# Float64 weights cut into high and low halves straight from their words, with the clamp on GpSimd, and 3 instead of 5 blocks of w_out in the attention stage

## The chip, the cores and the metric

The kernel runs on one core of a Trainium2 chip. The metric is the device time of one execution in microseconds (us), as the median of three runs. Profiles come from a separate, profiled execution; its own time is given beside its span. TensorE is PE in the profile, VectorE is DVE, ScalarE is ACT, GpSimd is POOL, and SP is the engine that issues most transfers.

## The reference

Three layers follow each other. A retention layer runs over 4 batches, 8 heads, 768 steps and 64 channels. A router then gives each of the 3072 tokens to one of 8 experts, 384 tokens each, in order of the logits, and an expert is two matrices with a ReLU between. Last comes a dense layer with softplus. The weights w_in and w_out of that last layer arrive as float64.

```
state = gamma * state + k_t v_t^T ;  y_t = scale * q_t state     # retention, 8 heads
order = argsort(-(x @ w_gate)) ; each token to its best expert with room (cap 384)
out[mask] = max(x[mask] @ w1[e], 0) @ w2[e]                      # expert e
h = x @ w_in ;  g = max(h, 0) + log1p(exp(-abs(h)))              # softplus
return (g @ w_out).astype(float32)
```

## The kernel before

**Stages.** The attention stage (`Attn.emit`) walks over 24 chunks of 128 tokens. Per chunk PE makes the scores (`qk`, tile `pA`), the output (`y`, tile `pY`), the state (`kv`, tile `pS`) and the transpose with the logits (`xo`, tile `pX`). DVE masks the scores (`at`, L125) and reduces the logits (`L`, L166). ACT evicts `yT`, `xs` and the state and scales the values (`vh`). POOL scales the queries (`qs`, L105), and SP loads and stores. Routing of the first expert follows, and then 8 experts, one after the other: `m1` and `m2` are the expert's two matrices, `f1` and `f2` the dense layer for the same 384 tokens. A float32 product is made of three products of a high and a low half, so each weight block has to be cut (`split_w`: ACT copies the high half `whi`, DVE subtracts for the low half `wlo`).

**The conversion.** The class `Conv` turns float64 words into float32. A float64 is loaded as two 32-bit words: `w0` is the lower one, `w1` the upper one with sign, exponent and 20 bits of the fraction (tile `raw`, two words side by side). `Conv.run` is a generator; each `yield` ends one step, and a step is one DVE instruction with what belongs to it on other engines. The first object works in the attention stage on blocks of 128 x 512 numbers: 16 blocks of w_in, each with two outputs (`wih` and `wil`, the high and low halves), and `kept` blocks of w_out with one output (`wo`). `side(j, part)` asks for steps at three places of a chunk: behind `at` of the next chunk, behind `y`, and at the chunk's end. A second object, `F.late`, works on the other rows of w_out in half blocks of 128 x 256. It takes 8 steps while the first list is routed, and then, in expert 0, 3 or 4 steps behind each item of the plan until it is through.

**The order.** All engines run in the order in which the code is written; nothing is rescheduled. Each engine has its own queue, in which a waiting instruction holds up those behind it.

**The steps before.** For one block: ACT writes the magnitude of `w1` to `cM` (L249), DVE shifts and masks `w1` into `cX` (L250), DVE puts the sign and the top exponent bit back (L256). One block later: DVE zeroes what is too small (L242), takes the exponent (L253), scales the lower word by it (L260) and adds (L269, into `cF`, or straight into `wo`). For blocks of w_in ACT then copies `cF` to the high half (L272), and DVE subtracts that for the low half (L263). The steps of two blocks are interleaved, so that most instructions do not need the result of the one just before them.

Of the kernel before, what the change touches and what calls it, by code (L numbers as in the profile page):

```python
# [9 lines left out]
FT = mybir.dt.float32  # L10
# [3 lines left out]
I32 = mybir.dt.int32  # L14
U32 = mybir.dt.uint32
AF = mybir.ActivationFunctionType
OP = mybir.AluOpType
# [19 lines left out]
def layouts(q, k, v, w1, w_in):  # L37

    B, H, S, D = q.shape
    T = lambda a: a.reshape(B, H // 2, 2, S // 128, 128, D).transpose(0, 3, 2, 5, 1, 4).reshape(-1, 128, 1, 512)  # L40
    R = lambda a: a.transpose(0, 2, 1, 3).reshape(-1, 128, 1, 512)
    qk = np.concatenate([T(q), T(k)], axis=2)
    kv = np.concatenate([R(k), R(v)], axis=2)
# [7 lines left out]
class Attn:  # L51
# [4 lines left out]
    def __init__(self, tc, ctx, ps, qk, kv, w_gate, tab, gqt, ident, L, xd, B, H, S):  # L56
        nc = self.nc = tc.nc
        self.ps = ps
        self.qk_in, self.kv_in, self.gq_in, self.L, self.xd, self.ident = qk, kv, gqt, L, xd, ident
        self.B, self.H, self.S = B, H, S  # L60
        self.NC = S // 128
        self.NCH = B * self.NC
        self.HP = HP = H // 2
        c = ctx.enter_context(tc.tile_pool(name="acst", bufs=1, side="right"))
        self.ld = ctx.enter_context(tc.tile_pool(name="ald", bufs=3, side="right"))
        self.wk = ctx.enter_context(tc.tile_pool(name="awk", bufs=2, side="right"))
        self.t = {}
        self.gq = c.tile([128, self.NC - 1, 512], FT, name="gqt")
        n = tab.shape[1] - 128
        ct = c.tile([128, n], FT, name="ctab")  # L70
        self.load(0, "qk")
        nc.scalar.dma_start(ct, tab[:, 128:])
        self.load(0, "kv")
        nc.scalar.dma_start(ident, tab[:, 0:128])
        self.cm = ct[:, 0:1024].rearrange("p (s a t) -> p s a t", s=2, a=HP)
        self.gk = ct[:, 1024:n].rearrange("p (c h) -> p c h", h=self.H)
        self.load(1)
        self.load(2)
        self.sb = []
        for i in range(2):  # L80
            self.sb.append(c.tile([128, HP, 128], FT, name=f"sbd{i}"))
        self.rx = c.tile([128, HP, 136], FT, name="rx")
        nc.scalar.dma_start(self.rx[:, :, 128:136], w_gate.rearrange("(a p) e -> p a e", p=128))
        self.pS = self.ps.tile([128, HP, 128], FT, name="pS")
# [122 lines left out]
        logits(n - 1)  # L207


TINY = float(np.array([897 << 20], np.int32).view(np.float32)[0])  # L210


class Conv:

    def __init__(self, tc, ctx, W, plan, bufs=3):
        self.nc, self.W, self.plan, self.bufs = tc.nc, W, plan, bufs
        self.st = ctx.enter_context(tc.tile_pool(name="cst", bufs=2, side="right"))
# [7 lines left out]
    def ahead(self, p=0):  # L227
        while self.loaded < min(p + self.bufs - 1, len(self.plan)):
            self.load(self.loaded)
            self.loaded += 1  # L230

    def run(self):

        nc, v, N = self.nc, self.nc.vector, len(self.plan)
        T = lambda name, dt, bufs: self.st.tile([128, self.W], dt, name=name, bufs=bufs)
        b, c = None, None
        for p in range(N + 2):
            self.ahead(p)
            a = None
            if b:  # L240
                q, m, x, l0 = b
                v.scalar_tensor_tensor(m, m, TINY, x.bitcast(FT), op0=OP.is_ge, op1=OP.mult)  # L242
                yield
            if p < N:
                raw = self.raw.pop(p)
                w0, w1 = raw[:, :, 0], raw[:, :, 1]
                M, X = T("cM", FT, 2), T("cX", I32, 2)
                a = p, M, X, w0
                nc.scalar.activation(M, w1.bitcast(FT), AF.Abs)  # L249
                v.tensor_scalar(X, w1, 3, 0x3fffffff, op0=OP.logical_shift_left, op1=OP.bitwise_and)  # L250
                yield
            if b:
                v.tensor_scalar(x, m.bitcast(I32), -0x800000, None, op0=OP.bitwise_and)  # L253
                yield
            if p < N:
                v.scalar_tensor_tensor(X, w1, -0x40000000, X, op0=OP.bitwise_and, op1=OP.bitwise_or)  # L256
                yield
            if b:
                e = x.bitcast(FT)
                v.scalar_tensor_tensor(e, l0.bitcast(U32), 2.0 ** -52, e, op0=OP.mult, op1=OP.mult)  # L260
                yield
            if c:
                v.tensor_tensor(c[1], c[0], c[2].bitcast(FT), op=OP.subtract)  # L263
                c = None
                yield
            if b:
                to = self.plan[q][1]
                F = to[0] if len(to) == 1 else T("cF", FT, 2)
                v.tensor_tensor(F, m, e, op=OP.add)  # L269
                if len(to) == 2:  # L270
                    f = F.rearrange("p (a n) -> p a n", a=4)
                    nc.scalar.activation(to[0], f, AF.Copy)  # L272
                    c = f, to[1], to[0]
                self.made += 1
                yield
            b = a

    def step(self, to=None):

# [15 lines left out]
class Route:  # L295
# [120 lines left out]
    def phase(self, i, slow=True, hum=lambda n: None, fill=lambda l: None):  # L416

        nc, N, E, w = self.nc, self.N, self.E, self.wp
        v = nc.vector
        T = lambda shape, dt, name, **k: w.tile(shape, dt, name=name, **k)  # L420
        gap = range
# [8 lines left out]
        for l, (J, s1, sh, span) in enumerate(() if last else LEVELS):  # L430
            if l:
                lo = T([128, N], I32, "lo")
                v.tensor_scalar(lo, self.ik, sh, span - 1, op0=OP.logical_shift_right, op1=OP.bitwise_and)
# [461 lines left out]
@with_exitstack  # L895
def model(ctx, tc, qk, kv, w_gate, w1, w2, w_in, w_out, tab, gqt, out, B, H, S):
    nc = tc.nc
    ctx.enter_context(tc.manual_schedule())
    nc.scalar.preload_act_table_set("natural_log_exp_and_others")
    pers = ctx.enter_context(tc.tile_pool(name="pers", bufs=1))  # L900
    dram = ctx.enter_context(tc.tile_pool(name="dram", bufs=1, space=bass.MemoryType.DRAM))
    NCH, E = 24, w1.shape[0]
    xd = dram.tile([NCH * 128, 512], FT, name="xd")
    L = pers.tile([128, NCH, E], FT, name="L")
    ident = pers.tile([128, 128], FT, name="identp")
    wih = pers.tile([128, 4, 2048], FR, name="wih")
    wil = pers.tile([128, 4, 2048], FR, name="wil")
    wo = pers.tile([128, 16, 512], FT, name="wo")
    holder = {}
    R = Route(tc, pers, None, lambda: holder["ps"](), L, NCH, E)  # L910
    w_in, w_out = w_in.bitcast(I32), w_out.bitcast(I32)
    c0, c1, c2 = (ctx.enter_context(ExitStack()) for _ in range(3))
    aps = c0.enter_context(tc.tile_pool(name="aps", bufs=1, space=bass.MemoryType.PSUM))
    cuts = [(w_in[f], (wih[:, :, f * 128:(f + 1) * 128], wil[:, :, f * 128:(f + 1) * 128])) for f in range(16)]
    kept = 5
    rows = [w_out[f * 128:(f + 1) * 128] for f in range(16)]
    cuts += [(rows[f], (wo[:, f],)) for f in range(kept)]
    cv = Conv(tc, c1, 512, cuts)
    a = Attn(tc, c2, aps, qk, kv, w_gate, tab, gqt, ident, L, xd, B, H, S)

    def side(j, part):
        cv.step((3 * j + part) * 144 // 71)

    def logits(j):
        if j % 6 == 5:
            R.first_part(j - 5, j + 1)

    a.emit(side, logits)
    cv.step(1000)
    c2.close()  # L930
    c1.close()
    R.wp = ctx.enter_context(tc.tile_pool(name="rwork", bufs=1, reuse_waits="tile"))
    holder["ps"] = lambda: a.ps.tile([128, 512], FT, name="pS")
    F = Ffn(tc, R, w1, w2, (wih, wil), [wo[:, f, :] for f in range(16)], xd, out, ident)
    F.open0(ctx)
    halves = [(rows[f][:, h * 512:h * 512 + 512], (wo[:, f, h * 256:h * 256 + 256],))
              for f in range(kept, 16) for h in range(2)]
    F.late, F.kept = Conv(tc, ctx, 256, halves, 3), kept
    F.start(a.ps.tile([128, 2, 4, 128], FT, name="pA", bufs=2)[:, 0].rearrange("p a t -> p (a t)"))
    c0.close()  # L940
    F.open(ctx)
    holder["ps"] = lambda: F.rps.tile([128, 512], FT, name="rt")
    F.emit()
# [25 lines left out]
```

## Time and profile before

| | |
|---|---|
| time, median of 3 runs | 1062.14 us (1061.06 to 1062.66) |
| profiled execution, its time | 1059.53 us |
| its span | 1057.8 us |
| PE busy | 1003.0 us (95%) |
| DVE busy | 694.6 us (66%) |
| ACT busy | 575.4 us (54%) |
| POOL busy | 84.1 us (8%) |

The shares are averages over stages with different limits, so they are to be read stage by stage. The attention stage ends near 144 us of the span, the routing of the first expert near 175 us, and the second conversion works until about 275 us. A busy share counts an instruction from its start to its end, also where it is held up inside; two instructions of one engine can overlap a little.

### The profile page before, as it was taken

The page shows a single profiled execution, that of the slowest core. Times are in us where ns is not written, and L with a number is a line of the kernel's source. Part 1 is how long each engine was busy: PE and PEld are TensorE (multiplying, and loading weights), DVE is VectorE, ACT ScalarE, POOL GpSimd, SP SyncE. Part 2 cuts the span into 40 slices and gives each one's busy share as a digit, 9 for nine tenths or more (in the row PEclk, how much of TensorE's full clock was granted, in tenths as well). Part 3 has the DMA queues.
Part 4 walks back from the last instruction along what each step waited for, and adds up shares of the span by engine and source line. Part 5 has one row for each costly group of instructions (what it writes and reads, how often), then busy time and mean ns, then how long its engine had stood idle before and what let it go on. Part 6 is the DMA issues. An engine that isn't in the chain of part 4 may idle for free.

```text
span 1057.8 us, 18750 instructions
## 1 busy us (share of the span) xinstructions
PE 1003.0 (95%) x7106; PEld 911.0 (86%) x7106; DVE 694.6 (66%) x1811; ACT 575.4 (54%) x1212; POOL 84.1 (8%) x110
## 2 busy tenths in 40 slices
PE   5998788988999999999999999999999999999997
PEld 5887766877889888989899989898988899999996
DVE  4999987998866666675667556756565744444442
ACT  4878722455543665366536653565356646564653
POOL 2221201000110101010001001100110020001001
PEclk9999999999999999999999999999999999999999
DMA  8989823421231102310141014100410150014000
GB/s 319 377 325 315 315 70 111 139 61 51 90 94 58 55 7 79 102 40 1 60 126 36 1 38 145 39 1 20 140 33 9 41 179 21 1 31 130 1 1 30
DMA packets 40458, 97.52 MB, mean 92 GB/s; under 512 B 5296, under 2 KB 5424, under 8 KB 40368
## 3 DMA queue, kind: packets, MB, share of 16 engines
q1 hardware_dynamic: 35712, 83.12, 24.0%
q0 software_dynamic: 3840, 12.59, 3.6%
q8 instruction: 55, 0.90, 0.3%
q10 hardware_dynamic: 816, 0.63, 0.2%
q14 instruction: 35, 0.29, 0.1%
HBM read 83.73 MB, written 12.58 MB: 91 GB/s over the span
## 4 chain that ended last, share of the span: by engine, by line
PE 66%; DVE 17%; issue 11%; ACT 2%; DMA 2%; POOL 1%; another core or an unknown queue 0%; ACTq 0%; POOLq 0%; DVEq 0%
PE h L660 11%; PE h L663 11%; PE h L661 10%; PE acc L758 7%; PE acc L759 7%; PE acc L763 7%; PE acc L652 3%; PE acc L654 3%; PE acc L653 3%; DVE at L125 2%; DVE cX L260 2%; PE rt L407 2%; DVE cM L242 2%; DVE cX L256 2%; DVE cX L250 1%
## 5 line engine op out<-in xcount | busy, mean ns | idle before, releaser
L724 DVE SCALAR_TENSOR_TENSOR gf<-h,sp 128x384 f32<-128x384 f32 x128 | 71.3, 557 | 189.2 <-ACT sp L722 189.2
L660 PE MATMUL h<-x2h,wih 128*128 128x384 f32 x512 | 177.1, 346 | 2.6 <-DVE xl L648 2.6
L661 PE MATMUL h<-x2h,wil 128*128 128x384 f32 x512 | 173.8, 339 | 0.0
L758 PE MATMUL acc<-whi,gh 128*128 128x512 f32 x384 | 153.7, 400 | 0.0
L759 PE MATMUL acc<-wlo,gh 128*128 128x512 f32 x384 | 151.4, 394 | 0.0
L720 ACT ACTIVATE sp<-h 128x384 f32<-128x384 f32 x128 | 62.6, 489 | 143.5 <-PE h L663 134.0
L663 PE MATMUL h<-x2l,wih 128*128 128x384 f32 x512 | 113.2, 341 | 0.9 <-DVE x2l L648 0.7
L763 PE MATMUL acc<-whi,gl 128*128 128x512 f32 x384 | 111.2, 396 | 0.0
L644 ACT ACTIVATE h1h<-h 128x384 fp32r<-128x384 f32 x64 | 31.5, 492 | 144.3 <-PE h L663 104.1
L660 PEld LDWEIGHTS h<-x2h,wih 128*128 128x128 f32 x512 | 97.0, 190 | 7.1 <-DVE xl L648 2.8
L661 PEld LDWEIGHTS h<-x2h,wil 128*128 128x128 f32 x512 | 97.2, 190 | 3.4
L663 PEld LDWEIGHTS h<-x2l,wih 128*128 128x128 f32 x512 | 91.9, 190 | 3.6 <-DVE x2l L648 3.6
L638 DVE TENSOR_TENSOR wlo<-wraw,whi 128x512 fp32r<-128x512 f32 x128 | 86.1, 687 | 6.9 <-ACT whi L637 6.9
L637 ACT ACTIVATE whi<-wraw 128x512 fp32r<-128x512 f32 x128 | 76.5, 624 | 25.2 <-DMA wraw<-in_moe_w_dram 23.3
L660 PE MATMUL h<-xh,whi 128*128 128x384 f32 x256 | 88.4, 345 | 0.7 <-ACT xh L647 0.7
L652 PE MATMUL acc<-h1h,whi 128*128 128x384 f32 x256 | 88.5, 346 | 0.0
L638 DVE TENSOR_TENSOR wlo<-wo,whi 128x512 fp32r<-128x512 f32 x128 | 87.4, 686 | 1.1 <-ACT whi L637 1.1
L763 PEld LDWEIGHTS acc<-whi,gl 128*128 128x128 f32 x384 | 72.0, 188 | 17.6 <-DVE gl L738 0.2
L654 PE MATMUL acc<-h1l,whi 128*128 128x384 f32 x256 | 86.2, 337 | 0.0
L653 PE MATMUL acc<-h1h,wlo 128*128 128x384 f32 x256 | 86.2, 337 | 0.0
L661 PE MATMUL h<-xh,wlo 128*128 128x384 f32 x256 | 86.2, 337 | 0.0
L645 DVE SCALAR_TENSOR_TENSOR h1l<-h,h1h 128x384 fp32r<-128x384 f32 x64 | 35.7, 557 | 74.5 <-ACT h1h L644 70.7
(202 smaller groups left out, 1889.4 us busy)
## 6 DMA issues: line engine op xcount, KB each, us to landing
wraw<-in_moe_w_dram SPq DMA_DIRECT2D x128, 256.0 KB, 2.7
qk_t<-in_qk_dram SPq DMA_DIRECT2D x24, 512.0 KB, 6.3
kv_t<-in_kv_dram SPq DMA_DIRECT2D x24, 512.0 KB, 5.4
raw<-in_moe_w_in_dram SPq DMA_DIRECT2D x16, 512.0 KB, 6.7
xd<-xs SPq DMA_DIRECT2D x24, 256.0 KB, 6.4
raw<-in_moe_w_out_dram SPq DMA_DIRECT2D x22, 256.0 KB, 2.8
raw<-in_moe_w_out_dram SPq DMA_DIRECT2D x5, 512.0 KB, 4.8
gqt<-in_gqt_dram SPq DMA_DIRECT2D x5, 256.0 KB, 6.0
```

Source lines behind the costliest of these rows:

```text
L637: nc.scalar.activation(hi, raw, AF.Copy)
L638: nc.vector.tensor_tensor(lo, raw, hi.bitcast(FT), op=OP.subtract)
L652: nc.tensor.matmul(ps, wh, ah, start=start, stop=False)
L653: nc.tensor.matmul(ps, wl, ah, start=False, stop=False)
L654: nc.tensor.matmul(ps, wh, al, start=False, stop=stop)
L660: mm(ps, wh(d), ah[:, d], start=d == 0, stop=False)
L661: mm(ps, wl(d), ah[:, d], start=False, stop=False)
L663: mm(ps, wh(d), al[:, d], start=False, stop=d == 3)
L724: nc.vector.scalar_tensor_tensor(g, ps, 0.0, a, op0=OP.max, op1=OP.add)
L758: nc.tensor.matmul(ps, gh[:, s], wh, start=f == 0, stop=False)
L759: nc.tensor.matmul(ps, gh[:, s], wl, start=False, stop=False)
L763: nc.tensor.matmul(ps, gl[:, s], wh, start=False, stop=f == 15)
```

## The change

The conversion clamps the magnitude of `w1` from below before anything is done with it, and no longer zeroes small values afterwards. ACT takes the magnitude into a tile `cA`, and POOL clamps it in place (`size`, a new function). That pair is issued one block ahead, in front of the fourth step of the block before it. For a block of w_in, DVE keeps the upper bits of the shifted word as the high half, which ACT copies out, and makes the low half from the remaining 9 bits and `w0` by two fused instructions; no full float32 value is made and subtracted from. That is 6 steps in place of 7. For a block of w_out it is 5 steps in place of 6. All steps of a block now follow each other; the blocks are no longer interleaved. The loads of raw words run one block further ahead. `kept` falls from 5 to 3, so the first object has 111 steps in place of 142 and is spread by 111/71 steps a place, and the second has 26 half blocks in place of 22, 130 steps in place of 132.

```diff
-TINY = float(np.array([897 << 20], np.int32).view(np.float32)[0])
+LEAST = float(np.array([896 << 20], np.int32).view(np.float32)[0])
+UPPER = -0x40000000
...
+    def size(self, p):
+        raw = self.raw.pop(p)
+        A = self.st.tile([128, self.W], I32, name="cA", bufs=2)
+        self.nc.scalar.activation(A.bitcast(FT), raw[:, :, 1].bitcast(FT), AF.Abs)
+        self.nc.gpsimd.tensor_scalar(A.bitcast(FT), A.bitcast(FT), LEAST, None, op0=OP.max)
+        return A, raw[:, :, 0].bitcast(U32), raw[:, :, 1]
...
+        self.ahead(0)
+        now = self.size(0)
+        for p in range(N):
+            self.ahead(p + 1)
+            A, w0, w1 = now
+            X, to = T("cX"), self.plan[p][1]
+            if len(to) == 2:
+                f = lambda t: t.rearrange("p (a n) -> p a n", a=4)
+                v.tensor_scalar(X, A, 3, 0x3ffff000, op0=OP.logical_shift_left, op1=OP.bitwise_and)
                 yield
+                v.scalar_tensor_tensor(X, w1, UPPER, X, op0=OP.bitwise_and, op1=OP.bitwise_or)
+                nc.scalar.activation(to[0], f(X.bitcast(FT)), AF.Copy)
                 yield
+                C = T("cC")
+                v.tensor_scalar(C, A, 0x1ff, 3, op0=OP.bitwise_and, op1=OP.logical_shift_left)
                 yield
+                if p + 1 < N:
+                    now = self.size(p + 1)
+                U = A.bitcast(FT)
+                v.scalar_tensor_tensor(U, w0, 2.0 ** -29, C, op0=OP.mult, op1=OP.add)
                 yield
+                v.tensor_scalar(C, X, -0x800000, None, op0=OP.bitwise_and)
                 yield
+                v.scalar_tensor_tensor(to[1], f(U), 2.0 ** -23, f(C.bitcast(FT)), op0=OP.mult, op1=OP.mult)
+            else:
+                v.tensor_scalar(X, A, 3, 0x3fffffff, op0=OP.logical_shift_left, op1=OP.bitwise_and)
                 yield
+                v.scalar_tensor_tensor(X, w1, UPPER, X, op0=OP.bitwise_and, op1=OP.bitwise_or)
                 yield
+                v.tensor_scalar(A, X, -0x800000, None, op0=OP.bitwise_and)
+                yield
+                if p + 1 < N:
+                    now = self.size(p + 1)
+                e = A.bitcast(FT)
+                v.scalar_tensor_tensor(e, w0, 2.0 ** -52, e, op0=OP.mult, op1=OP.mult)
+                yield
+                v.tensor_tensor(to[0], X.bitcast(FT), e, op=OP.add)
+            self.made += 1
+            yield
...
-    kept = 5
+    kept = 3
...
-        cv.step((3 * j + part) * 144 // 71)
+        cv.step((3 * j + part) * 111 // 71)
```

The first place is DVE in the attention stage, in the middle of the stage; `raw` are the loaded words, the brackets say which engine or queue the instruction waits for. Before, a chunk's stretch between two `at` read so:

```order
L125 TENSOR_TENSOR at<-pA,ctab 128x1024 [waits PE_49]
L253 TENSOR_SCALAR cX<-cM 128x512 [waits DVE_49]
L256 SCALAR_TENSOR_TENSOR cX<-raw,cX 128x512 [waits DVE_49]
L166 TENSOR_REDUCE L<-pX 128x8 [waits PE_49]
L260 SCALAR_TENSOR_TENSOR cX<-raw,cX 128x512 [waits DVE_49]
L263 TENSOR_TENSOR wil<-cF,wih 128x4x128 [waits Activation_49]
L269 TENSOR_TENSOR cF<-cM,cX 128x512 [waits DVE_49]
L242 SCALAR_TENSOR_TENSOR cM<-cM,cX 128x512 [waits Activation_49]
L125 TENSOR_TENSOR at<-pA,ctab 128x1024 [waits PE_49]
```

Now the stretch at the same place reads so (its line numbers are those of the changed file):

```order
L125 TENSOR_TENSOR at<-pA,ctab 128x1024 [waits PE_49]
L259 SCALAR_TENSOR_TENSOR cA<-raw,cC 128x512 [waits DVE_49]
L166 TENSOR_REDUCE L<-pX 128x8 [waits PE_49]
L261 TENSOR_SCALAR cC<-cX 128x512 [waits DVE_49]
L263 SCALAR_TENSOR_TENSOR wil<-cA,cC 128x4x128 [waits DVE_49]
L248 TENSOR_SCALAR cX<-cA 128x512 [waits Pool_49]
L250 SCALAR_TENSOR_TENSOR cX<-raw,cX 128x512 [waits DMAHW6_49,DVE_49]
L125 TENSOR_TENSOR at<-pA,ctab 128x1024 [waits PE_49]
```

Between two `at` there are five conversion steps in place of six, the first of a block (L248) waits for POOL, and two of the five (L263 and L250) use what the instruction just before them wrote.

The second place is POOL in the attention stage, from the sixth query scaling on. Before, its queue held nothing but the scalings L105; now the clamps L234 stand between them:

```order
L105 TENSOR_TENSOR qs<-qk_t,gqt 128x512 [waits DMAHW5_49,PE_49,Pool_49]
L234 TENSOR_SCALAR cA<-cA 128x512 [waits DVE_49,Activation_49]
L105 TENSOR_TENSOR qs<-qk_t,gqt 128x512 [waits DMAHW1_49,PE_49,Pool_49]
L234 TENSOR_SCALAR cA<-cA 128x512 [waits DVE_49,Activation_49]
L105 TENSOR_TENSOR qs<-qk_t,gqt 128x512 [waits DMAHW5_49,PE_49,Pool_49]
L105 TENSOR_TENSOR qs<-qk_t,gqt 128x512 [waits DMAHW1_49,PE_49,Pool_49]
L234 TENSOR_SCALAR cA<-cA 128x512 [waits DVE_49,Activation_49]
```

A clamp stands behind a scaling that waits for PE (the buffer of the scaling two chunks back) or for a load, and 19 of them come with the 20 scalings.

The third place is DVE in expert 0, where the half blocks stand among the weight halves (`wlo`), the hidden layer (`h1l`) and the routing of the next list. Before:

```order
L638 TENSOR_TENSOR wlo<-wraw,whi 128x512 [waits DMAHW3_49,Activation_49]
L269 TENSOR_TENSOR wo<-cM,cX 128x256
L242 SCALAR_TENSOR_TENSOR cM<-cM,cX 128x256
L250 TENSOR_SCALAR cX<-raw 128x256 [waits DMAHW4_49,DVE_49]
L253 TENSOR_SCALAR cX<-cM 128x256 [waits DVE_49]
L638 TENSOR_TENSOR wlo<-wraw,whi 128x512 [waits DMAHW5_49,Activation_49]
L645 SCALAR_TENSOR_TENSOR h1l<-h,h1h 128x384 [waits Activation_49]
```

Now:

```order
L640 TENSOR_TENSOR wlo<-wraw,whi 128x512 [waits DMAHW4_49,Activation_49]
L647 SCALAR_TENSOR_TENSOR h1l<-h,h1h 128x384 [waits Activation_49]
L274 SCALAR_TENSOR_TENSOR cA<-raw,cA 128x256 [waits DVE_49]
L276 TENSOR_TENSOR wo<-cX,cA 128x256 [waits DVE_49]
L265 TENSOR_SCALAR cX<-cA 128x256 [waits Pool_49]
L267 SCALAR_TENSOR_TENSOR cX<-raw,cX 128x256 [waits DMAHW3_49,DVE_49]
```

The steps behind an item are now steps of one block in a row, each of which needs the one before it, with the wait for POOL at the block's first.

## Rows read from the trace of the kernel before

**Rows 1.** The page, busy tenths in 40 slices of the span.

```profile
PE   5998788988999999999999999999999999999997
...
DVE  4999987998866666675667556756565744444442
```

**Rows 2.** Busy time by stretch: attention, expert 0 with conversion, the rest.

```profile
core 0: us, PE busy (x) PEld busy (x) DVE busy (x) ACT busy (x) POOL busy (x), PEclk, DMA share, GB/s
...
20.00:140.00 120.00, 104.78 (x1344) 94.18 (x1342) 119.33 (x221) 95.13 (x271) 26.03 (x18) 0.97 0.86 312
...
190.00:270.00 80.00, 71.55 (x513) 64.41 (x512) 73.61 (x233) 40.13 (x85) 2.89 (x3) 0.98 0.28 83
270.00:1058.00 788.00, 776.43 (x4834) 710.94 (x4832) 458.51 (x1185) 424.11 (x824) 46.27 (x67) 1.00 0.18 53
```

**Rows 3.** Groups of DVE by shape, 0 to 150 us: busy us, mean ns, idle.

```profile
L125 DVE TENSOR_TENSOR at<-pA,ctab 128x1024 f32<-128x1024 f32 x24 | 29.1, 1213 | 8.1 <-PE pA L124 8.1
L260 DVE SCALAR_TENSOR_TENSOR cX<-raw,cX 128x512 f32<-128x512 uint32 x21 | 16.6, 791 | 0.0
L242 DVE SCALAR_TENSOR_TENSOR cM<-cM,cX 128x512 f32<-128x512 f32 x21 | 15.2, 726 | 0.1
L256 DVE SCALAR_TENSOR_TENSOR cX<-raw,cX 128x512 int32<-128x512 int32 x21 | 14.3, 679 | 0.0
L263 DVE TENSOR_TENSOR wil<-cF,wih 128x512 fp32r<-128x512 f32 x16 | 13.4, 839 | 0.0
L269 DVE TENSOR_TENSOR cF<-cM,cX 128x512 f32<-128x512 f32 x16 | 12.5, 784 | 0.0
L250 DVE TENSOR_SCALAR cX<-raw 128x512 int32<-128x512 int32 x21 | 11.3, 538 | 4.5 <-DMA raw<-in_moe_w_in_dram 4.5
L253 DVE TENSOR_SCALAR cX<-cM 128x512 int32<-128x512 int32 x21 | 10.9, 518 | 0.0
L269 DVE TENSOR_TENSOR wo<-cM,cX 128x512 f32<-128x512 f32 x5 | 4.4, 885 | 0.1
```

**Rows 4.** Timeline of DVE near 103 us: start us, duration us, instruction.

```profile
103.23 0.68 DVE L242 SCALAR_TENSOR_TENSOR cM<-cM,cX 128x512 f32<-128x512 f32 x1
103.84 0.41 DVE L250 TENSOR_SCALAR cX<-raw 128x512 int32<-128x512 int32 x1
104.17 1.21 DVE L125 TENSOR_TENSOR at<-pA,ctab 128x1024 f32<-128x1024 f32 x1
```

**Rows 5.** Timeline of DVE near 192 us, in expert 0.

```profile
191.73 0.42 DVE L260 SCALAR_TENSOR_TENSOR cX<-raw,cX 128x256 f32<-128x256 uint32 x1
192.18 0.42 DVE L269 TENSOR_TENSOR wo<-cM,cX 128x256 f32<-128x256 f32 x1
```

**Rows 6.** Timeline of DVE and POOL near 115 us.

```profile
115.15 0.68 DVE L263 TENSOR_TENSOR wil<-cF,wih 128x512 fp32r<-128x512 f32 x1
...
115.50 1.47 POOL L105 TENSOR_TENSOR qs<-qk_t,gqt 128x512 f32<-128x512 f32 x1 [4.16 <-PE pY L133]
115.75 1.76 DVE L269 TENSOR_TENSOR cF<-cM,cX 128x512 f32<-128x512 f32 x1
```

**Rows 7.** Groups of POOL by shape, whole span.

```profile
L105 POOL TENSOR_TENSOR qs<-qk_t,gqt 128x512 f32<-128x512 f32 x20 | 28.6, 1429 | 97.0 <-PE pY L133 53.0 <-DMA qk_t<-in_qk_dram 41.2 <-issue 2.8
...
L91 POOL COPY rx<-identp 128x128 f32<-128x128 f32 x4 | 1.0, 296 | 0.0
L89 POOL MEMSET sbd<- 128x512 f32 x2 | 1.0, 526 | 0.0
```

**Rows 8.** Groups of DVE by shape, 145 to 330 us.

```profile
L256 DVE SCALAR_TENSOR_TENSOR cX<-raw,cX 128x256 int32<-128x256 int32 x22 | 9.2, 418 | 0.0
...
L250 DVE TENSOR_SCALAR cX<-raw 128x256 int32<-128x256 int32 x22 | 6.3, 286 | 0.0
```

**Rows 9.** Who waited for whom, 190 to 270 us: total, times, longest.

```profile
ACT cM L249 <- DVE wo L269: 27.6, 15, 3.6
...
DVE gf L724 <- ACT sp L722: 3.5, 7, 1.0
```

More of the change, by code (lines that the diff above doesn't have):

```diff
@@ L230, in ahead @@
             self.loaded += 1
+    def size(self, p):
[4 more added lines that the diff above has]
+        return A, raw[:, :, 0].bitcast(U32), raw[:, :, 1]
     def run(self):
         nc, v, N = self.nc, self.nc.vector, len(self.plan)
-        T = lambda name, dt, bufs: self.st.tile([128, self.W], dt, name=name, bufs=bufs)
@@ L236, in run @@
[L236 to L242, printed above, removed]
-                yield
[L244 to L250, printed above, removed]
+        T = lambda name: self.st.tile([128, self.W], I32, name=name, bufs=2)
@@ L251, in run @@
                 yield
-            if b:
-                v.tensor_scalar(x, m.bitcast(I32), -0x800000, None, op0=OP.bitwise_and)
+                C = T("cC")
+                v.tensor_scalar(C, A, 0x1ff, 3, op0=OP.bitwise_and, op1=OP.logical_shift_left)
                 yield
-            if p < N:
-                v.scalar_tensor_tensor(X, w1, -0x40000000, X, op0=OP.bitwise_and, op1=OP.bitwise_or)
+                if p + 1 < N:
+                    now = self.size(p + 1)
+                U = A.bitcast(FT)
@@ L257, in run @@
+                v.scalar_tensor_tensor(U, w0, 2.0 ** -29, C, op0=OP.mult, op1=OP.add)
                 yield
-            if b:
-                e = x.bitcast(FT)
-                v.scalar_tensor_tensor(e, l0.bitcast(U32), 2.0 ** -52, e, op0=OP.mult, op1=OP.mult)
+                v.tensor_scalar(C, X, -0x800000, None, op0=OP.bitwise_and)
                 yield
-            if c:
-                v.tensor_tensor(c[1], c[0], c[2].bitcast(FT), op=OP.subtract)
-                c = None
+                v.scalar_tensor_tensor(to[1], f(U), 2.0 ** -23, f(C.bitcast(FT)), op0=OP.mult, op1=OP.mult)
+            else:
+                v.tensor_scalar(X, A, 3, 0x3fffffff, op0=OP.logical_shift_left, op1=OP.bitwise_and)
@@ L265, in run @@
                 yield
[L266 to L274, printed above, removed]
-                yield
-            b = a
+                v.scalar_tensor_tensor(X, w1, UPPER, X, op0=OP.bitwise_and, op1=OP.bitwise_or)
```

## The prediction

> **What bounds the kernel now.** I read the busy slices first. They show two regions where DVE is full and PE is not, the first three or so tenths of the span, and a long rest where PE is full and DVE half idle [rows 1]. The change touches nothing in that rest: from 270 us on PE is busy for 776 of 788 us [rows 2], and its matmuls stay as they are. So the sum is made of two stretches only.
>
> The table of stretches sizes both. In the attention stage, 20 to 140 us, DVE is busy for 119.3 of 120 us, PE for 104.8, and the DMA engines for 0.86 of the time, which is 103 us [rows 2]. DVE sets the pace there, with two others some 15 us behind. In expert 0, while the half blocks are converted, 190 to 270 us, DVE is busy for 73.6 of 80 us and PE for 71.6 [rows 2]. There nobody is full; DVE and PE wait for each other in turn, and DVE has 6.4 us to spare.
>
> **Prices on DVE.** An undisturbed instruction with two inputs in SBUF takes 0.68 us for 512 columns, and the next one starts 0.60 us after it; a tensor_scalar takes 0.41 and gives way after 0.33 [rows 4]. For 256 columns the rows have 418 and 286 ns [rows 8]; less the same overlap of 0.08 that is 0.34 and 0.20. Where an instruction needs the result of the one just before it, the overlap is lost: the add at 192.18 starts 0.03 us after the end of the product at 191.73 [rows 5], 0.11 us more than the usual 0.08 of overlap. The new instructions have the shapes and places of old ones (the product of the lower word with a second tile is like L260, the low half written in four pieces is like L263), so I give them these prices.
>
> **Attention stage, what goes.** A block of w_in had 5 two-input instructions and 2 tensor_scalars, 5 x 0.60 + 2 x 0.33 = 3.66 us; a block of w_out 4 and 2, 3.06 us. Sixteen and five of them make 73.9 us, with 6 dependent neighbours 74.5. The new block of w_in has 3 and 3, 2.79 us, the new one of w_out 3 and 2, 2.46 us; sixteen and three make 52.0. In the order of the change I count 44 neighbours where the second waits for the first (9 of them only because it overwrites what the first reads), 44 x 0.11 = 4.8, together 56.8 us. That takes **17.7 us** from DVE.
>
> **Attention stage, what comes.** Nineteen clamps of 512 columns on POOL. No row shows a clamp. From below stands the memset of 512 columns, 526 ns, which only writes; from above the scaling with two inputs, 1429 ns [rows 7]. One input and one output lie nearer to the memset: I take 0.75. POOL has time for it, but DVE pays too. The add at 115.75 took 1.76 us in place of 0.68, 1.08 more, while POOL scaled from 115.50 to 116.97 [rows 6]. Over the stage the means of the eight groups of the conversion stand above 0.68 and 0.41 by 13.5 us in all (21 x 0.11 + 21 x 0.05 + 16 x 0.16 + 16 x 0.10 + 21 x 0.13 + 21 x 0.11 + 5 x 0.20, L256 nothing) [rows 3]. With 20 scalings that is 0.67 us each, 0.47 of a scaling's 1.43; the rest fell on instructions that are not held up, such as `at`, which reads PSUM and has the same 1.21 us alone [rows 4] as in the mean of all 24 [rows 3]. At the same share a clamp costs DVE 0.35, and as Abs ends at any moment, not mostly beside `at` as the scalings do, I take 0.40: 19 x 0.40 = **7.6 us**, between 19 x 0.25 = 4.7 (memset) and 19 x 0.67 = 12.7. It could be below that, down to nothing, only where DVE stands still anyway, waiting for that clamp.
>
> The Trainium skill has a rule that speaks against a clamp on this engine: SBUF — State Buffer, section Who interferes with whom, says that GpSimd and such DVE instructions share a pair of ports that is locked for a whole instruction, and the loser blocks fully. The disturbed add agrees in kind. By the rule alone each clamp would cost its full 0.75, 14 us in the stage; the rows say that about half of that reaches DVE.
>
> So DVE's work falls by 17.7 - 7.6 = 10.1, to 109.2 us. The stage can't follow it all the way: PE has 104.8 and the DMA engines 103 minus two loads, so three resources come within 6 us of each other, and what PE now loses waiting for DVE it then loses partly to ACT. I give back 4 of the 10: **the stage gets 6 us shorter**. The bounds are 10 (all of it) and 0 (next paragraphs).
>
> The new wait in this stage is that a block's first step waits for ACT's Abs and POOL's clamp, issued three steps earlier. Behind that step on DVE stand `at` and the logits; PE needs `at` a full chunk later, so a stall below 1 us there does no harm while DVE has slack. POOL's queue holds the clamp behind a scaling that waits for PE, 53.0 us in 20 scalings, or for a load [rows 7]; but those waits end early in the chunk in which they are issued. I price this at nothing; the cover is that chunk of slack, and without it 19 blocks x 0.5 us = 9.5 us would eat the gain.
>
> **Expert 0.** Before, 88 two-input instructions and 44 tensor_scalars, 29.9 + 8.8 = 38.7, and 21 dependent neighbours, 41.0 us. Now 78 and 52, 26.5 + 10.4 = 36.9, but 77 dependent neighbours, 8.5, together 45.4: **4.4 us more**, though two blocks more cost hardly anything by themselves. The 26 clamps of 256 columns have the copy of 128 columns (296 ns) [rows 7] below them and half a scaling, 0.71, above; I take 0.42. At 0.47 to 0.73 of it (the 1.08 of 1.47 in [rows 6], as no `at` stands here to take it) DVE pays 0.27: **7.0 us**, between 26 x 0.14 = 3.6 and 26 x 0.52 = 13.5. Eight of the 130 steps lie in the routing before, 0.7 us. DVE so gets 10.7 more, 84.3 us in a stretch of 80.
>
> Of the 6.4 us that DVE idles now, part is ACT's doing: Abs stands in ACT's queue until the add two blocks back has freed its tile, 27.6 us in 15 waits [rows 9], and weight halves and activations queue behind it, for which DVE then waits, as in the 3.5 us for softplus [rows 9]. The new Abs takes a tile that is free three steps earlier, so this coupling loosens. I let 5.7 of the 6.4 be used up: **the stretch gets 5 us longer**, with 4.3 (all idle filled) to 10.7 (none) as its ends at this price.
>
> **Sum.** The profiled execution took 1059.53 us, 1.7 of it outside the span of 1057.8, and is 2.6 below the median of 1062.14. -6 + 5 = -1 on either: 1058.5 for an execution like the profiled one, **1061** for the median. About 0.2%, 2.1 us, is what a measurement of this kernel can tell from no change.
>
> **Rivals.** *Slower: the lock in expert 0 costs its whole length.* A clamp starts when Abs ends, and Abs follows the activation that DVE was also waiting for, so it hits the conversion steps in a row every time. It speaks for this that these steps have two SBUF inputs or are tensor_scalars, all kinds that were held up in [rows 3]. Against it: L256 was not held up in 21 cases. At 0.42 for each of 26 it is 10.9 in place of 7.0, DVE has 88.2 us, the stretch grows by 9; with 4 gained in attention the time is 1067. It decides from 0.35 us a clamp on. *Faster: expert 0 absorbs it.* If a clamp locks DVE for 0.14, DVE has 80.9 us of work there and, with the looser ACT queue, the stretch grows by 2; the attention stage then also pays only 4.7, loses 13 of DVE's time and gains 8. That gives 1056. Speaking against it: dependent neighbours alone use up 4.4 of the 6.4 us. *The attention stage doesn't shorten.* Blocks wait 0.5 us for their clamps behind ACT's eight `vh`, the 6 us gain is gone and expert 0's 5 us remain: 1067 too, so I count it with the first.
>
> **How the numbers follow.** Forecast 0.45 (own range 1057 to 1065), the slower cases 0.33, the faster one 0.22. Of the forecast's 0.45 I put 0.18 below 1060, 0.23 within 2.1 us of the old time and 0.04 above. With nearly all of the rivals on their own side: faster 0.39, same 0.26, slower 0.35. The range 1054 to 1069 takes in both rivals with about 2 us around them.
>
> **What the new profile should show.** DVE's conversion groups in the attention stage with about 57 us of undisturbed work and means above 0.68 and 0.41 by some 21 us in all (13.5 + 7.6); clamps of 0.53 to 1.0 us; the last `xo` some 6 us earlier; DVE no longer at 99% there. In expert 0 DVE above 95% busy between its first and last half block, ACT's wait for the add gone, and that stretch 5 us longer. What would make it wrong: clamps well over 1 us, DVE waiting for POOL by more than 5 us in all, or PE or a load pacing the attention stage with no gain left.

## The result

| | before | after |
|---|---|---|
| time, median of 4 runs each | 1061.78 us (1061.06 to 1062.66) | 1074.46 us (1072.06 to 1077.22) |
| ratio, 95% interval | | 1.0120 (1.0094 to 1.0146) |
| profiled execution, its time | 1059.53 us | 1077.22 us |
| its span | 1057.8 us | 1075.5 us |
| last matmul of the attention output (`pY`, L138) starts at | 139.3 us | 151.2 us |
| first weight load of expert 0's dense layer (`f1`, L660; L662 in after) starts at | 217.3 us | 233.9 us |
| last one of that line, in the last expert, starts at | 1042.9 us | 1060.7 us |

The change made the kernel 12.7 us slower, beyond the end of the predicted range, 1069. The three marks in the table say where; they stand in these lines, of before and of after (count, shortest/median/longest ns, first and last start):

```profile
L138 PE MATMUL pY<-at,kv_t x384: 272/273/477, 12.4 to 139.3; 128*64 128x128 f32 x192
L660 PEld LDWEIGHTS h<-x2h,wih x512: 187/188/334, 217.3 to 1042.9; 128*128 128x128 f32 x171
...
L138 PE MATMUL pY<-at,kv_t x384: 272/273/476, 12.5 to 151.2; 128*64 128x128 f32 x192
L662 PEld LDWEIGHTS h<-x2h,wih x512: 186/188/334, 233.9 to 1060.7; 128*128 128x128 f32 x171
```

The attention stage ends 11.9 us later, the stretch from there to expert 0's dense layer is 4.7 us longer (82.7 in place of 78.0), and the long rest 1.2 us longer. Over all kernels of this document that rest takes from 823.4 to 830.9 us, so its 1.2 us tell nothing. The profiled execution of after lies 2.8 us above its median and that of before 2.3 below, so these parts add up to more than the medians differ.

The page of after, busy tenths in 40 slices, answers to [rows 1]:

```profile
PE   4888787988899999999999999999999999999997
...
DVE  4788977798986656675667566655675754354442
POOL 3343331122301010100011001100101020001001
```

Of DVE's row of nines in the first slices one is left (the fifth slice), and PE has no such row there either. The stretches say it in numbers. They answer to [rows 2], and the second one lies 15 us later because the whole stage does:

```profile
core 0: us, PE busy (x) PEld busy (x) DVE busy (x) ACT busy (x) POOL busy (x), PEclk, DMA share, GB/s
...
20.00:140.00 120.00, 98.29 (x1220) 89.89 (x1220) 101.84 (x174) 87.42 (x250) 47.54 (x35) 0.93 0.85 290
...
205.00:285.00 80.00, 69.32 (x494) 62.12 (x493) 73.82 (x217) 38.34 (x83) 18.87 (x21) 0.96 0.28 87
285.00:1075.00 790.00, 778.74 (x4854) 712.70 (x4852) 464.00 (x1199) 426.52 (x830) 51.63 (x73) 1.00 0.18 54
```

In the attention stage DVE is busy for 101.8 of 120 us, 17.5 less than before, PE for 98.3 in place of 104.8, and ACT for 87.4 in place of 95.1. None of the three is full, and each does less in the same 120 us, so they wait for one another. In expert 0 DVE has 73.8 of 80 us, as before (73.6).

The groups of POOL by shape show the clamps (L234) beside the scalings (L105); behind the bar stands the idle time of POOL ahead of them, and what ended it:

```profile
L234 POOL TENSOR_SCALAR cA<-cA 128x512 f32<-128x512 f32 x19 | 28.6, 1503 | 83.8 <-ACT cA L233 73.3 <-DVE wil L263 5.5 <-PE pS L151 5.0
L105 POOL TENSOR_TENSOR qs<-qk_t,gqt 128x512 f32<-128x512 f32 x20 | 26.2, 1311 | 9.4 <-DMA qk_t<-in_qk_dram 8.7 <-PE pY L133 0.4 <-POOL qs L105 0.2
...
L234 POOL TENSOR_SCALAR cA<-cA 128x256 f32<-128x256 f32 x26 | 23.4, 902 | 95.9 <-ACT cA L233 87.5 <-DMA raw<-in_moe_w_out_dram 8.4
```

A clamp of 512 columns takes 1.50 us, double the 0.75 that I took and above my upper bound. POOL had time for it: it stood idle for 83.8 us ahead of these 19 clamps, 73.3 of them until ACT's Abs (L233) was through. Who waits for whom in the attention stage, 20 to 145 us (total, times, longest):

```profile
POOL cA L234 <- ACT cA L233: 69.5, 16, 6.8
...
DVE cX L248 <- POOL cA L234: 18.7, 10, 6.8
PE pX L163 <- ACT yT L141: 16.2, 10, 4.0
ACT wih L251 <- DVE cX L250: 14.9, 11, 3.0
```

POOL waits for ACT, DVE for POOL, ACT for DVE again, and PE for ACT. DVE's 18.7 us are blocks of w_in; blocks of w_out wait another 2.7 us, in two waits, up to the end of the stage. The last two of these waits were there before as well, in the same stretch:

```profile
PE pX L163 <- ACT yT L141: 11.8, 11, 3.0
ACT wih L272 <- DVE cF L269: 9.8, 8, 2.5
```

One turn of it stands in the timeline near 43 us (start, duration, engine, instruction; in brackets how long the engine had stood idle, and for whom):

```profile
40.87 2.02 ACT L113 ACTIVATE vh<-kv_t,ctab 128x64 f32<-128x64 f32 x8
41.08 0.68 DVE L263 SCALAR_TENSOR_TENSOR wil<-cA,cC 128x512 fp32r<-128x512 f32 x1
41.68 0.18 DVE L166 TENSOR_REDUCE L<-pX 128x8 f32<-128x32 f32 x1
...
42.80 0.67 ACT L233 ACTIVATE cA<-raw 128x512 f32<-128x512 f32 x1
...
43.55 1.48 POOL L234 TENSOR_SCALAR cA<-cA 128x512 f32<-128x512 f32 x1 [5.68 <-ACT cA L233]
...
45.07 0.43 DVE L248 TENSOR_SCALAR cX<-cA 128x512 int32<-128x512 int32 x1 [3.20 <-POOL cA L234]
45.53 0.69 DVE L250 SCALAR_TENSOR_TENSOR cX<-raw,cX 128x512 int32<-128x512 int32 x1
...
46.25 0.63 ACT L251 ACTIVATE wih<-cX 128x512 fp32r<-128x512 f32 x1 [1.68 <-DVE cX L250]
...
46.79 0.76 ACT L156 ACTIVATE sbd<-pS 64x256 f32<-64x256 f32 x2
...
47.65 1.13 PE L133 MATMUL pY<-qs,sbd 128*128 128x128 f32 x8 [1.62 <-issue]
```

DVE has done its last step of the old block at 41.76, and the logits at 41.86, and then needs the clamped block. But Abs stands behind the eight `vh` in ACT's queue, starts at 42.80, and the clamp follows until 45.03: DVE stands still for 3.20 us. Then the wait goes on to ACT and PE. The copy of the high half (L251) has meanwhile come to the head of ACT's queue and waits 1.68 us for DVE; behind it stands `sbd`, the evicted state, which PE's next product reads. PE stands still for 1.62 us, which the profile puts down to `issue`, and goes on 0.1 us after `sbd` has ended.

The groups of DVE by shape, 0 to 150 us (busy us, mean ns, idle), answer to [rows 3]:

```profile
L125 DVE TENSOR_TENSOR at<-pA,ctab 128x1024 f32<-128x1024 f32 x24 | 29.2, 1218 | 12.0 <-PE pA L124 12.0
L248 DVE TENSOR_SCALAR cX<-cA 128x512 int32<-128x512 int32 x16 | 16.3, 1016 | 18.7 <-POOL cA L234 18.7
L250 DVE SCALAR_TENSOR_TENSOR cX<-raw,cX 128x512 int32<-128x512 int32 x16 | 15.0, 936 | 0.3
L263 DVE SCALAR_TENSOR_TENSOR wil<-cA,cC 128x512 fp32r<-128x512 f32 x16 | 14.4, 898 | 0.3
L259 DVE SCALAR_TENSOR_TENSOR cA<-raw,cC 128x512 f32<-128x512 uint32 x16 | 12.8, 800 | 0.2
L261 DVE TENSOR_SCALAR cC<-cX 128x512 int32<-128x512 int32 x16 | 7.5, 471 | 0.3
L254 DVE TENSOR_SCALAR cC<-cA 128x512 int32<-128x512 int32 x16 | 6.7, 416 | 0.0
...
L265 DVE TENSOR_SCALAR cX<-cA 128x512 int32<-128x512 int32 x2 | 3.0, 1491 | 0.4 <-POOL cA L234 0.4
```

Over the undisturbed 0.68 and 0.41 they stand by 16 x 0.61 + 16 x 0.26 + 16 x 0.22 + 16 x 0.12 + 16 x 0.06 + 2 x 1.08 = 22.5 us, where 21 were predicted. The total came out close, but not what it is made of. Nine of the 16 L248 and two L265 take 1.41 to 1.50 us, each beside the scaling that POOL had queued right behind the clamp; these eleven make about 11.8 of the 22.5 us. The 18.7 us of standing still come on top.

### The profile page after: what moved, and what is told of

It is laid out like the page before. It is cut to its first block, busy times and chain, and to the rows that moved or that the text cites. A ratio compares the mean times of both kernels' runs of the same rounds, so it can differ in the third digit from the quotient of the medians.

```text
span 1075.5 us, 18792 instructions
## 1 busy us (share of the span) xinstructions
PE 1008.1 (94%) x7106; PEld 916.8 (85%) x7106; DVE 692.4 (64%) x1778; ACT 575.8 (54%) x1214; POOL 132.8 (12%) x155
## 4 chain that ended last, share of the span: by engine, by line
PE 67%; issue 13%; DVE 12%; DMA 3%; POOL 2%; ACT 2%; SPq 0%; POOLq 0%; ACTq 0%; DVEq 0%
PE h L662 11%; PE h L665 10%; PE h L663 10%; PE acc L760 7%; PE acc L761 7%; PE acc L765 7%; PE acc L654 3%; PE acc L656 3%; PE acc L655 3%; PE rt L409 2%; DMA qk_t<-in_qk_dram 2%; DVE wlo L640 1%; PE h L686 1%; PE pX L163 1%; POOL cA L234 1%
## 5 line engine op out<-in xcount | busy, mean ns | idle before, releaser
L662 PE MATMUL h<-x2h,wih 128*128 128x384 f32 x512 | 176.4, 345 | 2.2 <-DVE xl L650 2.2
L646 ACT ACTIVATE h1h<-h 128x384 fp32r<-128x384 f32 x64 | 31.4, 491 | 151.2 <-PE h L665 113.4
L662 PEld LDWEIGHTS h<-x2h,wih 128*128 128x128 f32 x512 | 96.6, 189 | 8.0 <-DVE xl L650 2.4
L662 PE MATMUL h<-xh,whi 128*128 128x384 f32 x256 | 89.6, 350 | 0.7 <-ACT xh L649 0.7
L773 POOL DMA_INDIRECT out_dram<-rows,ix x24 | 25.3, 1056 | 513.2 <-ACT rows L771 509.8
```

What stands on the lines that cost most here:

```text
L662: mm(ps, wh(d), ah[:, d], start=d == 0, stop=False)
```

## The experiments

Three theories stood at the start. **W**: DVE waits for the chain of Abs and clamp. **L**: POOL's clamps hold DVE's instructions up, whoever waits for them. **M**: the blocks moved into expert 0, and the steps that now follow each other directly, cost it. All kernels are the changed one with one edit, except `e6_old_kept3`. Times are medians. A ratio is against the kernel before on the same chip, with its 95% interval; it can differ from the quotient of the two medians by up to 0.3%. The marks come from one profiled execution each.

### Without the clamp

The clamp is left out everywhere, so values below the smallest magnitude are not raised.

```diff
         self.nc.scalar.activation(A.bitcast(FT), raw[:, :, 1].bitcast(FT), AF.Abs)
-        self.nc.gpsimd.tensor_scalar(A.bitcast(FT), A.bitcast(FT), LEAST, None, op0=OP.max)
```

> The changed kernel without the clamp in both stages: DVE's first step of a block takes ACT's magnitude as it is. Left out: numbers below the smallest normal float32 are not treated. Theory W (DVE waits for the chain Abs, clamp) and theory L (the clamp locks DVE out of SBUF while it runs) both expect the clamp to be nearly the whole loss: 1074 less 17 or more, 1053 to 1058, with the last mask of the attention stage at or before 132 us. Theory M (the moved blocks and the steps that each need the one before) expects 1066 or more.

Measured: 1050.94 us, ratio 0.9887 (0.9848 to 0.9927). The last `pY` starts at 129.9, 9.4 us ahead of before. So the steps themselves and the moved blocks are worth some 12 us by the ratio, M falls as the cause, and all of the loss hangs on the clamp.

### The clamp on DVE

```diff
+            v.tensor_scalar(A.bitcast(FT), A.bitcast(FT), LEAST, None, op0=OP.max)
             X, to = T("cX"), self.plan[p][1]
```

(in place of the line on POOL).

> The changed kernel with the clamp moved to DVE, as one more tensor_scalar at the front of each block (19 of 0.33 us, 26 of 0.20, with a dependent neighbour each). Theories W and L: about 12 us of DVE work more than without any clamp, of which part is hidden, so 1058 to 1064; POOL's lock and the wait are gone. Theory M: 1070 or more.

Measured: 1064.35 us, ratio 1.0025 (1.0002 to 1.0049). On the engine that was to be relieved the clamp costs some 13 us over the kernel without it, and still 10 us less than on POOL.

### The clamp without the wait

In the attention stage POOL does as much as after, but on a tile of its own, behind a copy of one column from `cA`; DVE reads `cA` as Abs leaves it, so the blocks of this stage are not clamped.

```diff
...
-        self.nc.gpsimd.tensor_scalar(A.bitcast(FT), A.bitcast(FT), LEAST, None, op0=OP.max)
+        if self.W == 512:
+            self.nc.gpsimd.tensor_copy(self.D[:, 0:1], A.bitcast(FT)[:, 0:1])
+            self.nc.gpsimd.tensor_scalar(self.D, self.D, LEAST, None, op0=OP.max)
+        else:
+            self.nc.gpsimd.tensor_scalar(A.bitcast(FT), A.bitcast(FT), LEAST, None, op0=OP.max)
```

> In the attention stage alone, POOL still runs a clamp of 512 columns per block at the same place and released by the same Abs, but on a tile of its own; DVE reads the unclamped magnitude and waits for POOL no more. Expert 0 is as in the changed kernel. Left out: the clamp's effect in the attention stage. Theory W: the stage comes back by most of its loss, 1074 becomes 1058 to 1064. Theory L: the lock stays, so the time stays at 1070 or more, with the groups of the conversion as far above 0.68 and 0.41 as in the changed kernel.

Measured: 1058.35 us, ratio 0.9980 (0.9956 to 1.0005). DVE no longer waits for POOL at all in the stage, and what is left of the other waits (20 to 145 us) is:

```profile
POOL cD L238 <- ACT cA L236: 50.3, 17, 6.3
...
PE pX L163 <- ACT yT L141: 11.1, 11, 3.1
...
ACT wih L258 <- DVE cX L257: 4.3, 4, 2.5
```

POOL still waits for Abs, which harms nobody now. The clamps are there and even longer, 1.70 us by the group of that kernel's POOL, and the attention stage ends at 136.0:

```profile
L239 POOL TENSOR_SCALAR cD<-cD 128x512 f32<-128x512 f32 x19 | 32.3, 1701 | 1.7
...
L138 PE MATMUL pY<-at,kv_t x384: 272/273/476, 12.8 to 136.0; 128*64 128x128 f32 x192
```

So the wait, not the work on POOL, makes 16.1 us of the kernel's time (1074.46 - 1058.35; 14.9 by the ratios). What POOL's work costs besides is priced below, by the clamp in expert 0 alone.

### Two blocks ahead

Abs and clamp are issued two blocks ahead in the attention stage, with a third `cA` and a fourth `raw` tile.

```diff
...
-                if p + 1 < N:
-                    now = self.size(p + 1)
+                if p + k < N:
+                    now.append(self.size(p + k))
...
```

> In the attention stage alone, Abs and clamp are issued two blocks ahead in place of one, with a third magnitude tile and a fourth tile of raw words, so that DVE finds its clamp done; the clamps still run and lock. Theory W: nearly as without the wait, 1058 to 1064, DVE's waits for POOL below 3 us in place of 18.7. Theory L: 1070 or more. If both count, between.

Measured: 1062.09 us, ratio 1.0016 (0.9996 to 1.0037). DVE's wait for POOL shrinks to 6.8 us, once, at the first block. After that block the wait is gone with the clamp's whole work intact, and with it 12 us; 4 more separate it from the kernel above. The last `pY` starts at 139.7, no earlier than before.

### Five blocks, as before

```diff
-    kept = 3
+    kept = 5
...
-        cv.step((3 * j + part) * 111 // 71)
+        cv.step((3 * j + part) * 121 // 71)
```

> The changed kernel with five blocks of w_out in the attention stage again (121 steps spread by 121/71). Theory W: each further block in the stage waits for its clamp too, and expert 0 gets four half blocks fewer, so the two about cancel, 1070 to 1080. Theory M (the moved blocks cost): 1069 or less.

Measured: 1080.46 us, ratio 1.0201 (1.0161 to 1.0241); the last `pY` starts at 159.7, 8.5 us after that of after. Two blocks more in the stage make it worse, so moving them out was no part of the loss. The blocks of w_out wait for their clamps as well, 10.5 us in five waits, where in after it is 2.7 in two.

### Three blocks in the kernel before

```diff
-    kept = 5
+    kept = 3
...
-        cv.step((3 * j + part) * 144 // 71)
+        cv.step((3 * j + part) * 132 // 71)
```

> The kernel before with only the move: three blocks of w_out in the attention stage, 26 half blocks in expert 0, old steps (128 for two blocks fewer, spread by 132/71). DVE has 2 x 3.1 us less in a stage that it fills and 4 x 1.8 us more in expert 0. Theory W (the move is not the cause): 1058 to 1064. Theory M: 1069 or more.

Measured: 1060.45 us, ratio 0.9997 (0.9975 to 1.0018). Alone, the move changes nothing that can be measured. M is settled.

### The clamp in expert 0 alone

The blocks of the attention stage are not clamped.

```diff
-        self.nc.gpsimd.tensor_scalar(A.bitcast(FT), A.bitcast(FT), LEAST, None, op0=OP.max)
+        if self.W == 256:
+            self.nc.gpsimd.tensor_scalar(A.bitcast(FT), A.bitcast(FT), LEAST, None, op0=OP.max)
```

> The changed kernel with the clamp in expert 0 alone; in the attention stage DVE takes ACT's magnitude as it is. Left out: the clamp's effect in the attention stage. Beside the run without any clamp (1050.9) it prices the 26 clamps of expert 0; beside the run with POOL's clamp on a tile of its own (1058.4) it prices the lock in the attention stage. The rows of those runs let the stage end at 136.0 with the lock and 129.9 without: 1051 to 1054. If expert 0's clamps cost their whole length as I had it in the slower rival (0.42 us each and more), 1058 or more.

Measured: 1053.68 us, ratio 0.9937 (0.9911 to 0.9963). The 26 clamps of half blocks cost 2.7 us by the medians, 5 by the two ratios, whose intervals overlap; the stretch from the last `pY` to expert 0's dense layer is no longer with them (77.6 against 79.9 in `e1_no_clamp`), so where they cost is not shown. The 19 clamps of whole blocks without their wait then make the 4.7 us from here to 1058.35, and the wait the rest. These two intervals overlap by a hair too, but the mark agrees: the stage ends at 129.9 here and 6.1 us later with those clamps. L is true in kind, and smaller than the wait.

```profile
L138 PE MATMUL pY<-at,kv_t x384: 272/273/476, 12.4 to 129.9; 128*64 128x128 f32 x192
```

### Abs and clamp two steps earlier

`size(p + 1)` is issued behind a block's first step in place of its third, for both kinds of block.

```diff
                 v.tensor_scalar(X, A, 3, 0x3ffff000, op0=OP.logical_shift_left, op1=OP.bitwise_and)
+                if p + 1 < N:
+                    now = self.size(p + 1)
                 yield
...
-                if p + 1 < N:
-                    now = self.size(p + 1)
                 U = A.bitcast(FT)
```

(and the same in the branch of w_out).

> The changed kernel with Abs and clamp of the next block issued behind the first step of a block in place of the third, in both stages, with the same tiles; the clamp stays on POOL and counts. Theory W: the wait goes for the most part, the lock stays, near the run with the clamp on its own tile, 1057 to 1064. If ACT, which now waits at Abs for the last step of the block before, holds up the rest of its queue, 1065 to 1074.

Measured: 1062.60 us, ratio 1.0019 (0.9998 to 1.0040). DVE's wait for POOL is 6.8 us at the first block, and 0.4 at one block of w_out. No third tile is needed; two steps are enough.

Here two theories about the 16 us parted: **stall**, it is only DVE's standing still; **loop**, a part is ACT's copy L251, which waits for the standing DVE with PE's evictions behind it. The next three kernels move the copy, Abs and clamp, or both.

### The copy behind the fifth step

```diff
                 v.scalar_tensor_tensor(X, w1, UPPER, X, op0=OP.bitwise_and, op1=OP.bitwise_or)
-                nc.scalar.activation(to[0], f(X.bitcast(FT)), AF.Copy)
...
                 v.tensor_scalar(C, X, -0x800000, None, op0=OP.bitwise_and)
+                nc.scalar.activation(to[0], f(X.bitcast(FT)), AF.Copy)
```

> The changed kernel with one line moved: ACT's copy of the high half is issued behind the fifth step of a block in place of the second. DVE still waits for its clamp. Theory loop (DVE's wait hurts because ACT's copy then waits for DVE at the head of ACT's queue, and the yT that PE needs stands behind it): the time falls by 5 us or more, 1062 to 1069, and ACT's waits for the copy, 14.9 us, nearly go. Theory stall (DVE's own standing still is the whole loss): within 3 us of 1074.

Measured: 1069.45 us, ratio 1.0068 (1.0049 to 1.0087), 5.0 us under after by the medians: at the very edge of what the loop theory had expected, and outside the 3 us of the stall theory. The copy's own wait is no longer among the waits (20 to 145 us), and DVE's for POOL is shorter, though it stays:

```profile
PE pX L163 <- ACT yT L141: 19.1, 14, 3.0
...
DVE cX L248 <- POOL cA L234: 13.8, 6, 6.8
```

But PE's wait for `yT`, by which the copy was to harm PE, is 19.1 us here against 16.2 in after. So the 5 us did not come back by that wait, and the way by which they did is open.

### Earlier for w_in only

The edit of `e8_early` in the branch of w_in alone.

> The changed kernel with Abs and clamp issued behind the first step for the blocks of w_in only; blocks of w_out and expert 0 as in the changed kernel. The stage then ends as with the early clamp everywhere (last pY at 134.6) and expert 0 as with the clamp on its own tile: 1057 to 1061, where the early clamp everywhere gave 1062.6. If the early position in expert 0 was not what cost there, 1061 to 1064.

Measured: 1062.26 us, ratio 1.0004 (0.9990 to 1.0018). DVE waits 6.8 us at the first block and 2.3 at one block of w_out. Within its interval it is the time before, and that of `e8_early`; where Abs stands in expert 0 makes no difference that was measured. The last `pY` starts at 137.4, 2.8 us later than in `e8_early`, though the blocks of w_in have the same code; blocks of w_out differ. ACT's copy hardly waits any more, though nobody moved it:

```profile
ACT wih L253 <- DVE cX L252: 2.6, 2, 1.4
```

### Both

The edits of `e9_copy_late` and `e10_early_att` together.

> As the run with the early clamp for w_in, and ACT's copy behind the fifth step. Theory loop: little is left to gain, as DVE waits no more, 0 to 3 us below that run, 1055 to 1060, which would be below both kernels. If the late copy delays the block's second half (ACT reads the tile longer), 1 to 3 us above it.

Measured: 1059.64 us, ratio 0.9971 (0.9954 to 0.9988), 0.3% under the kernel before and 1.5% under after by the ratios, with every clamp in place. The waits, 20 to 145 us:

```profile
POOL cA L234 <- ACT cA L233: 63.2, 16, 8.2
...
PE pX L163 <- ACT yT L141: 9.3, 10, 1.8
...
DVE cX L248 <- POOL cA L234: 6.8, 1, 6.8
...
DVE cX L265 <- POOL cA L234: 2.9, 2, 2.3
```

The four combinations stand side by side:

| ratio to before | copy behind the second step | copy behind the fifth |
|---|---|---|
| Abs and clamp in front of the fourth step | 1.0120 (after) | 1.0068 |
| Abs and clamp behind the first step (w_in) | 1.0004 | 0.9971 |

Earlier Abs is worth 1.2% or 1.0%, the later copy 0.5% or 0.3%, both together 1.5%, 16 us: as much as the clamp without the wait had promised. So the larger part, some 1%, is what an early Abs takes away whether the copy is moved or not. The loop theory, by contrast, is not shown. It needs the copy to cost more while DVE stands still, and 0.5% and 0.3% differ by less than their intervals allow to tell (each ratio is known to 0.14 to 0.26%). A later copy helps; that it helps because of the stall is only argued.

## Why the prediction was wrong

**The step that failed** is the new wait in the attention stage, which I priced at nothing: "the cover is that chunk of slack, and without it 19 blocks x 0.5 us = 9.5 us would eat the gain". The cover was looked for at the wrong end. PE does need `at` only a chunk later, but what decides is whether the chain is through when DVE comes to the block's first step. Between issue and use DVE has only three conversion steps and at most one `at`, and in that time Abs has to pass what ACT's queue holds (eight `vh`, 2.02 us), run (0.67), and be clamped (1.48). Ten blocks of w_in were late, by 18.7 us in all; without the first block, which waits 6.8 us in `e11_early_att_copy_late` as well, it is 11.9 us in nine waits. Taking these waits away by issuing earlier gave 12.3 us by the ratios (1.0120 - 1.0004). The clamp's length has its part in it: five of the nine waits are between 1.28 and 3.20 us and four at most 0.55, so with 0.75 us less for each clamp, the price that I had taken, they would add up to 6.5 in place of 11.9, by an estimate that leaves the rest as it is.

**What I did not see** is where such a wait goes on to: the stalled DVE in turn stalls ACT's copy, 14.9 us in eleven waits in place of 9.8 in eight, and ACT's queue holds what PE needs. How much of the loss goes that way is not shown. The rival that came nearest, that the attention stage doesn't shorten because blocks wait for their clamps, had the place right, but priced the wait at 0.5 us a block and with nothing behind it, and so ended at 1067. Two of the signs that I had named for being wrong are met: DVE waits for POOL by more than 5 us in all, and the clamps take well over 1 us.

**What held.** The attention stage can get shorter once DVE hardly waits, though by less than the 6 us predicted: it ends 3.3 us earlier than before in `e3_lock_only` (last `pY` 136.0 against 139.3), 4.7 in `e8_early` and `e11_early_att_copy_late` (134.6) and 1.9 in `e10_early_att`, but 0.4 later in `e4_two_ahead`. The total of `e3_lock_only`, 2.1 us under before by its ratio where I had -1, is partly luck: by its marks it is made of -3.3 in the attention stage, +0.5 up to expert 0's dense layer and +1.7 in the rest, not of -6 and +5. DVE's price for the clamps has to be read against `e1_no_clamp`, which has the same steps and POOL's scalings alone: its groups stand 11.1 us above 0.68 and 0.41, those of `e3_lock_only` 19.0, so the clamps cost 7.9 us of DVE's time for the 7.6 predicted. That too is partly luck, since each clamp is twice as long as I took it, and its share that reaches DVE is thus about half of what I reckoned with. In after, where some of a clamp falls while DVE stands still and the next scaling catches DVE instead, it is 22.5 - 11.1 = 11.4.

**Mis-sized.** The clamp of 512 columns: 1.50 in place of 0.75 us, and outside the bounds of 0.53 to 1.43; that of 256 columns 0.90 against an upper bound of 0.71. Expert 0's clamps cost DVE hardly anything: its groups of the half blocks, 145 to 340 us, stand at

```profile
L267 DVE SCALAR_TENSOR_TENSOR cX<-raw,cX 128x256 int32<-128x256 int32 x26 | 11.4, 440 | 0.6
L274 DVE SCALAR_TENSOR_TENSOR cA<-raw,cA 128x256 f32<-128x256 uint32 x26 | 11.2, 429 | 0.7
...
L276 DVE TENSOR_TENSOR wo<-cX,cA 128x256 f32<-128x256 f32 x26 | 11.0, 423 | 0.7
L269 DVE TENSOR_SCALAR cA<-cX 128x256 int32<-128x256 int32 x26 | 8.4, 324 | 0.7
L265 DVE TENSOR_SCALAR cX<-cA 128x256 int32<-128x256 int32 x26 | 7.4, 285 | 0.0
```

against 418 and 286 undisturbed [rows 8]: 26 x (0.022 + 0.011 + 0.005 + 0.038) = 2.0 us, where I had 7.0. DVE there is busy for 92%, not above 95, and ACT's wait for the add two blocks back is not gone but down from 27.6 us [rows 9] to 17.2 in ten waits (185 to 290 us). The rule that I weighed in the prediction (the Trainium skill, SBUF — State Buffer, section Who interferes with whom: the loser of the shared ports blocks fully) would by itself give up to 19 x 1.50 = 28.5 us of DVE's time in the attention stage. The trace agrees in kind (L248 with 1.49 us in the last section); the clamps' cost to DVE came out at 7.9 to 11.4 us, and the kernel's time shows 4.7 from `e7_late_clamp` to `e3_lock_only`.

**What stays open.** The stretch between the last `pY` and expert 0's dense layer took 78.0 us before. Six kernels have after's conversion code in expert 0, and took 77.7 (`e4_two_ahead`), 78.5 (`e3_lock_only`), 79.2 (`e9_copy_late`), 81.9 (`e10_early_att`), 82.4 (`e11_early_att_copy_late`) and 82.7 us (after). Whether the predicted 5 us longer is right is not settled by that. With the copy late, the late Abs costs 10.3 us (1.0068 - 0.9971), of which DVE's waits beyond the first block make only 7.0 (13.8 - 6.8); where the rest is lost was not followed further. TensorE's granted clock, a mean over its levels of 1.2 and 2.4 GHz, was 0.93 of full speed in the attention stage of after (0.97 before [rows 2]), 0.94 in `e10_early_att` and 0.97 in `e11_early_att_copy_late`; part of what the copy costs may go through it, which no run shows.

## What to carry to other kernels

A helper on other engines that is put ahead of a step is priced by each queue that it passes: what stands in front of it there, how long it runs, and how much the waiting engine has to do between issue and use. If that is close, issue it some steps earlier before judging the idea, and look what the stalled engine holds up in turn in other in-order queues. A kernel in which the consumer reads unprocessed data, while the helper does its work beside it, tells the price of the wait from that of the work in one run.

## What the runs showed of the hardware

The one-input clamp of 512 columns on POOL takes longer (1503 ns) than the product of two inputs of the same shape (1311), though I had taken it for something nearer to a memset. From the means of its two shapes, by an estimate, (1503 - 902) / 256 = 2.3 ns a column and some 0.3 us that don't depend on the size.

The clamp takes longer where DVE works beside it: 1.48 us at 43.55, where DVE stands still, and 1701 ns in the mean of `e3_lock_only`, where DVE hardly waits. That DVE holds POOL up is the likely reading; no run takes it by itself. And an instruction of DVE that the clamp has just released can be caught by the next one on POOL. In after's timeline near 50 us:

```profile
50.06 1.26 POOL L105 TENSOR_TENSOR qs<-qk_t,gqt 128x512 f32<-128x512 f32 x1
...
50.12 1.49 DVE L248 TENSOR_SCALAR cX<-cA 128x512 int32<-128x512 int32 x1 [0.36 <-POOL cA L234]
```

L248 takes 1.49 us in place of 0.41, the same 1.08 more as the add in [rows 6], and ends 0.29 us after the scaling.
